# Two DMA queues for x and B, x transposed between the halves of B, and y one gate step later, in a fused state-space and gated-FFN kernel

## The chip, the cores and the metric

The kernel runs on one core of one Trainium2 chip. The metric is the time of one execution on the device in microseconds (us). A profiled run also has a span, from the first to the last instruction that the profile counts, which is about 2 us shorter. Every execution is sorted as fast or slow by its time and granted clock, and only fast ones are compared; the state of a single execution is unknown. Engines are named as in the profile: PE (matrix engine), DVE (vector), ACT (scalar), POOL (GpSimd) and SP (sync, which issues most DMAs).

## The reference, cut to what matters

```python
xn = _layernorm(x)                              # 2048 tokens x 512
Bu = xn @ B_bar.T                               # complex, 512 states
h[t] = Lam_bar * h[t-1] + Bu[t]                 # complex recurrence over 2048 tokens
s  = 2 * real(h @ C.T) + xn * Dskip
g  = silu((gelu(xn @ w_gate) * (xn @ w_up)) @ w_down)     # width 1376
out = x + s * g
```

## The kernel before

The tokens are worked in four slabs of 512. In each slab PE makes eight groups `u` (B times xn), which DVE rotates, scans and rotates back into `hst`; eleven gate steps `g_ps`, `up_ps`; four groups `f` (the down projection); and four groups `y` from `hst` (C times h). The `y` of slab s-1 stand between the gate steps of slab s, at the steps `Y_AT`. All tiles in PSUM, the memory that PE writes its results to, are taken in turn from eight buffers under one tag, so each PE group waits until the reader of the tile eight places earlier is done.

```python
psum = ctx.enter_context(tc.tile_pool(name="psum", bufs=8, space=bass.MemoryType.PSUM))
...
def ffn(s, j, at):                     # one gate step
    ...                                # 4 matmuls into g_ps, 4 into up_ps
    ACT(out=gt[:fs], in_=g_ps[:fs, :], func=AF.Gelu_apprx_tanh)
    ACT(out=ub[:fs], in_=u_ps[:fs, :], func=AF.Copy)
    dve(now() + 0.9, 0.34, lambda: TT(out=at[:fs, j, :], in0=gt[:fs], in1=ub[:fs], op=ALU.mult))
def down(s, m, at):
    ...                                # 11 matmuls into f_ps; ACT makes th = tanh(f/2)
    dve(now() + 0.9, 0.6, lambda: STT(out=g2[:], in0=th[:], scalar=1.0, in1=f_ps[:, :], op0=ALU.add, op1=ALU.mult))
def epi(s, m, y_ps, g2):
    ...                                # DVE: yg = y_ps * g2; ot = yg + x
    nc.sync.dma_start(out=out_td[mg : mg + P, :], in_=ot[:])
def ln_small(s):                       # 7 POOL instructions on 128x4: mean, variance, rs, nb
def ln_out(s, m):                      # ACT: xn = rs*x + nb; SP: DMA transpose of xn into xnT
...
for j in range(NFT):                   # slab s > 0
    ffn(s, j, ats[s])
    if s < NS - 1:
        if j < M: ln_act(s + 1, j)     # sums of the next slab's rows, on ACT
        if j == M - 1: ln_small(s + 1)
        if 5 <= j < 5 + M: ln_out(s + 1, j - 5)
    if j in Y_AT: ...                  # y of slab s-1 and its epilogue
```

DVE's instructions are ordered when the program is built, by a small model of PE's and DVE's clocks: `dve(ready, cost, f)` places an instruction at a modelled time, with the queued scans and rotations put in ahead of it where they fit. A model that is wrong costs time at run time, because the order is fixed.

## Time and profile before

| | before |
|---|---|
| time, median of 4 fast runs | 190.67 us (190.26 to 191.15) |
| span of the profiled run | 188.8 us |
| PE, DVE, ACT, POOL busy | 96%, 88%, 57%, 12% |
| first `u` matmul | 10.94 us |
| gaps of PE over 0.2 us after it | one: the first `y` of slab 1 (1.34 us lost) |

The page of the kernel before has, in its first part, the busy time of each engine (share of the span, number of instructions), and in its fourth part the engines' shares of the chain that ended last:

```profile
PE 181.2 (96%) x918; PEld 85.9 (45%) x918; DVE 165.5 (88%) x284; ACT 108.0 (57%) x202; POOL 21.7 (12%) x35
...
PE 89%; ACT 4%; DMA 2%; DVE 2%; SPq 1%; issue 0%
...
L431 DVE TENSOR_TENSOR at<-gt,ub 128x512 bf16<-128x512 bf16 (+1 forms) x44 | 18.2, 416 | 4.2 <-ACT ub L430 4.0
```

The last line is from the costliest groups: busy time, mean ns, and then the idle time of DVE just before these instructions, here 4.2 us, 4.0 of them ended by ACT's copy `ub`. PE rules the chain; DVE works 88% of the time.

### The profile page before, as it was taken

How to read it: one execution, taken by the hardware profiler on the slowest of the kernel's cores; microseconds unless marked ns; L12 is line 12 of the kernel's file. 1: busy time of each engine (PE TensorE's matmuls, PEld its weight loads, DVE VectorE, ACT ScalarE, POOL GpSimd, SP SyncE). 2: the span in 40 equal slices, each digit the busy share in tenths (PEclk: the TensorE clock that was granted, in tenths of full speed). 3: DMA queues.
4: the chain of work that ended last, by engine and by line, in shares of the span. 5: the costliest groups of instructions: out<-in, count | busy, mean ns of one | idle time of the engine just before them, and what ended most of it. 6: DMA issues, size and time to landing. Idle time of an engine off the chain costs nothing.

```text
span 188.8 us, 2587 instructions
## 1 busy us (share of the span) xinstructions
PE 181.2 (96%) x918; PEld 85.9 (45%) x918; DVE 165.5 (88%) x284; ACT 108.0 (57%) x202; POOL 21.7 (12%) x35
## 2 busy tenths in 40 slices
PE   7789999999999799999999999999999999999992
PEld 2444444444444244544444444544444444554452
DVE  4879799999999897999999999999999999973353
ACT  3399989995259919536239959537226644321210
POOL 3737200000000470000000080000000000000000
PEclk9999999999999999999999999999999999999999
DMA  5999948700000003300000003300000000000001
GB/s 131 343 363 360 233 110 254 109 3 0 0 0 0 0 3 84 82 28 28 0 5 0 0 2 83 87 28 28 0 0 0 3 0 28 28 28 31 28 30 56
DMA packets 21164, 12.26 MB, mean 65 GB/s; under 512 B 11456, under 2 KB 21152, under 8 KB 21152
## 3 DMA queue, kind: packets, MB, share of 16 engines
q1 hardware_dynamic: 20976, 12.03, 23.7%
q8 instruction: 7, 0.11, 0.2%
q10 hardware_dynamic: 176, 0.07, 0.1%
q14 instruction: 5, 0.04, 0.1%
HBM read 7.38 MB, written 2.10 MB: 50 GB/s over the span
## 4 chain that ended last, share of the span: by engine, by line
PE 89%; ACT 4%; DMA 2%; DVE 2%; SPq 1%; issue 0%
PE f_ps L438 20%; PE up_ps L423 18%; PE g_ps L418 18%; PE u_ps L333 15%; PE y_ps L457 14%; DMA Bn<-in_A_B_re_dram 2%; ACT junk L512 2%; PE y_ps L462 2%; PE tb_ps L140 1%; ACT ub L430 1%; PE y_ps L490 1%; SPq L89 1%; ACT gt L428 1%; DVE qq L352 1%; DVE xnT L212 0%; DVE hst L356 0%
## 5 line engine op out<-in xcount | busy, mean ns | idle before, releaser
L418 PE MATMUL g_ps<-xnT,wg 128*128 128x512 bf16 (+1 forms) x176 | 45.2, 379 | 0.0
L423 PE MATMUL up_ps<-xnT,wu 128*128 128x512 bf16 (+1 forms) x176 | 45.2, 379 | 0.0
L438 PE MATMUL f_ps<-wd,at 128*128 128x512 bf16 (+1 forms) x176 | 38.7, 379 | 0.0
L428 ACT ACTIVATE gt<-g_ps 128x512 bf16<-128x512 f32 (+1 forms) x44 | 26.0, 592 | 13.2 <-PE g_ps L418 13.2
L382 DVE TENSOR_TENSOR_SCAN Ft<-rho,it,Wt 128x512 bf16<-128x512 f32 x24 | 30.3, 1276 | 0.0
L457 PE MATMUL y_ps<-C,hst 128*128 128x512 bf16 x120 | 28.7, 379 | 1.0 <-DVE hst L356 1.0
L430 ACT ACTIVATE ub<-up_ps 128x512 bf16<-128x512 f32 (+1 forms) x44 | 26.3, 598 | 5.1 <-PE up_ps L423 5.1
L333 PE MATMUL u_ps<-xnT,BT 128*128 128x512 bf16 x128 | 28.3, 379 | 0.6 <-DVE xnT L212 0.6
L443 ACT ACTIVATE th<-f_ps 128x512 f32<-128x512 f32 x16 | 9.6, 598 | 32.3 <-PE f_ps L438 30.5
L423 PEld LDWEIGHTS <-wu 128*128 128x128 bf16 (+1 forms) x176 | 17.6, 100 | 20.4
L438 PEld LDWEIGHTS <-at 128*128 128x128 bf16 (+1 forms) x176 | 17.1, 98 | 20.6
L418 PEld LDWEIGHTS <-wg 128*128 128x128 bf16 (+1 forms) x176 | 17.2, 100 | 18.4
L338 ACT ACTIVATE U<-u_ps 128x512 bf16<-128x512 f32 x32 | 17.7, 602 | 8.3 <-PE u_ps L333 8.3
L431 DVE TENSOR_TENSOR at<-gt,ub 128x512 bf16<-128x512 bf16 (+1 forms) x44 | 18.2, 416 | 4.2 <-ACT ub L430 4.0
L333 PEld LDWEIGHTS <-BT 128*128 128x128 bf16 x128 | 12.4, 98 | 15.1 <-issue 0.7
L457 PEld LDWEIGHTS <-hst 128*128 128x128 bf16 x120 | 11.5, 98 | 15.1 <-DVE hst L356 2.0
L445 DVE SCALAR_TENSOR_TENSOR g<-th,f_ps 128x512 f32<-128x512 f32 x16 | 10.9, 679 | 7.6 <-ACT th L443 7.6
L527 ACT ACTIVATE xn<-x_tok,nb,rs 128x512 bf16<-128x512 bf16 x12 | 9.8, 814 | 6.1 <-POOL nb L523 6.1
L475 DVE TENSOR_TENSOR yg<-y_ps,g 128x512 bf16<-128x512 f32 x15 | 10.3, 684 | 1.9 <-PE y_ps L462 1.8
L356 DVE TENSOR_TENSOR Wt<-pp,qq 128x1024 bf16<-128x1024 bf16 x16 | 10.8, 688 | 0.3
L356 DVE TENSOR_TENSOR hst<-pp,qq 128x1024 bf16<-128x1024 bf16 x16 | 10.6, 689 | 0.2
L517 POOL TENSOR_SCALAR sx<-sx 128x4 f32<-128x4 f32 x2 | 1.4, 684 | 81.2 <-ACT junk L512 81.2
(108 smaller groups left out, 166.6 us busy)
## 6 DMA issues: line engine op xcount, KB each, us to landing
out_dram<-ot SPq DMA_DIRECT2D x15, 128.0 KB, 1.7
x_tok<-in_A_x_dram SPq DMA_DIRECT2D x3, 512.0 KB, 4.1
wd<-in_B_w_down_dram SPq DMA_DIRECT2D x1, 1280.0 KB, 11.3
x_tok<-in_A_x_dram SPq DMA_DIRECT2D x4, 128.0 KB, 2.4
Bn<-in_A_B_re_dram SPq DMA_DIRECT2D x1, 512.0 KB
Bn<-in_A_B_im_dram SPq DMA_DIRECT2D x1, 512.0 KB, 5.6
wg<-in_B_w_gate_dram SPq DMA_DIRECT2D x1, 512.0 KB, 8.2
wu<-in_B_w_up_dram SPq DMA_DIRECT2D x1, 512.0 KB
```

What stands on the lines that cost most here:

```text
L333: nc.tensor.matmul(u_ps[:, :], lhsT=BT[:, ri, kt, pt * P : (pt + 1) * P], rhs=xnT[:, kt, cols], start=(kt == 0), stop=(kt == KT - 1),)
L338: ACT(out=U[:, ri, q, :], in_=u_ps[:, :], func=AF.Copy)
L356: return lambda: TT(out=dst()[i], in0=box["pp"][:, i, :, :], in1=box["qq"][:, 1 - i, :, :], op=op)
L382: nc.vector.tensor_tensor_scan(out=box["F"][:, ri, q, :], data0=rho[:, pt : pt + 1].to_broadcast([P, TS]), data1=box["W"][:, ri, q, :], in ...
L418: nc.tensor.matmul(g_ps[:fs, :], lhsT=wg[:, kt, fsl], rhs=xnT[:, kt, cols], start=(kt == 0), stop=(kt == KT - 1))
L423: nc.tensor.matmul(u_ps[:fs, :], lhsT=wu[:, kt, fsl], rhs=xnT[:, kt, cols], start=(kt == 0), stop=(kt == KT - 1))
L428: ACT(out=gt[:fs], in_=g_ps[:fs, :], func=AF.Gelu_apprx_tanh)
L430: ACT(out=ub[:fs], in_=u_ps[:fs, :], func=AF.Copy)
L431: dve(now() + 0.9, 0.34, lambda: TT(out=at[:fs, j, :], in0=gt[:fs], in1=ub[:fs], op=ALU.mult))
L438: nc.tensor.matmul(f_ps[:, :], lhsT=at[:fs, k, m0 : m0 + P], rhs=wd[:fs, k, :], start=(k == 0), stop=(k == NFT - 1))
L445: dve(now() + 0.9, 0.6, lambda: STT(out=g2[:], in0=th[:], scalar=1.0, in1=f_ps[:, :], op0=ALU.add, op1=ALU.mult))
L457: nc.tensor.matmul(y_ps[:, :], lhsT=hst[:, j // NPT, j % NPT, m0 : m0 + P], rhs=C2[:, j // NPT, j % NPT, :], start=(j == 0), stop=False,)
```

## The change

It is meant to fill DMA capacity that lies unused at the start, to let DVE's work on x overlap the loads of B, and to give DVE one gate step more for `hst` before the first two `y`.

```diff
-    for m in range(M):
-        nc.sync.dma_start(out=x_tok[:, m, :], in_=x_r[:, m, :])
+    nc.sync.dma_start(out=x_tok[:, 0, :], in_=x_r[:, 0, :])
+    nc.sync.dma_start(out=x_tok[:, 1, :], in_=x_r[:, 1, :])
+    nc.sync.dma_start(out=x_tok[:, 2:M, :], in_=x_r[:, 2:M, :])
+    load_b(nc.sync, 1, A_B_im)
     for i, v in enumerate((A_log_dt, A_Lambda_im, A_Lambda_re, A_Dskip)):
         nc.scalar.dma_start(...)
-    for ri, src in enumerate((A_B_re, A_B_im)):
-        nc.sync.dma_start(out=Bn[:, ri, :, :], ...)
+        if i == 1:
+            load_b(nc.scalar, 0, A_B_re)
...
-    dummies(10) ... dummies(3)
+    dummies(12)
+    b_transposes(0)
...  (statistics and norms of x; x0 and x1 transposed; the parameters transposed)
+    b_transposes(1)
     nc.vector.tensor_copy(out=pf[:], in_=pt_ps[:, :])
...  (norms of x2, x3; copies to xnT; the angle chain now after them)
-    Y_AT = (5, 7, 9, 10)
+    Y_AT = (6, 8, 9, 10)
...
-    clk["pe"] = 9.5
+    clk["pe"] = 9.0
```

The last line is the start of the modelled clock.

More of the change, by code (lines that the diff above doesn't have):

```diff
@@ L87, with load_b @@
     wu_r = B_w_up.rearrange("(k p) f -> p k f", p=P)
-    for m in range(M):
-        nc.sync.dma_start(out=x_tok[:, m, :], in_=x_r[:, m, :])
+    def load_b(eng, ri, src):
+        eng.dma_start(out=Bn[:, ri, :, :], in_=src.rearrange("(k p) d -> p k d", p=P))
+    nc.sync.dma_start(out=x_tok[:, 0, :], in_=x_r[:, 0, :])
+    nc.sync.dma_start(out=x_tok[:, 1, :], in_=x_r[:, 1, :])
+    nc.sync.dma_start(out=x_tok[:, 2:M, :], in_=x_r[:, 2:M, :])
+    load_b(nc.sync, 1, A_B_im)
     for i, v in enumerate((A_log_dt, A_Lambda_im, A_Lambda_re, A_Dskip)):
         nc.scalar.dma_start(out=pv[4 * i : 4 * i + 4, :], in_=v.rearrange("(k p) -> k p", p=P))
-    for ri, src in enumerate((A_B_re, A_B_im)):
-        nc.sync.dma_start(out=Bn[:, ri, :, :], in_=src.rearrange("(k p) d -> p k d", p=P))
+        if i == 1:
+            load_b(nc.scalar, 0, A_B_re)
     cuts = [0, 3 * P, 7 * P, F]
@@ L181 @@
     ch = consts.tile(W3, BF16, name="ch")
-    dummies(10)
+    dummies(12)
+    b_transposes(0)
+    for a in (0, 2):
+        for m in (a, a + 1):
+            bn(0, m)
+        for m in (a, a + 1):
+            bn_end(0, m)
+        rstd(0, a, a + 2)
+    xs = [norm0(0), norm0(1)]
+    tps = [t_xn0(0, xs[0]), t_xn0(1, xs[1])]
     pt_ps = psum.tile([P, 16], BF16, name="pt_ps", tag="ps")
     nc.tensor.transpose(pt_ps[:, :], pv[:, :], ident[0:16, 0:16])
-    dummies(3)
-    bn(0, 0)
-    bn(0, 1)
-    bn_end(0, 0)
-    bn_end(0, 1)
-    rstd(0, 0, 2)
-    bn(0, 2)
+    b_transposes(1)
     nc.vector.tensor_copy(out=pf[:], in_=pt_ps[:, :])
     nc.gpsimd.tensor_tensor(out=dt_[:], in0=euler[:], in1=ldt, op=ALU.pow)
-    bn(0, 3)
-    bn_end(0, 2)
-    bn_end(0, 3)
-    rstd(0, 2, 4)
-    xs = [norm0(0), norm0(1)]
-    STT(out=thn[:], in0=lim, scalar=1.0 / (2.0 * math.pi), in1=dt_[:], op0=ALU.mult, op1=ALU.mult)
-    TT(out=a1[:], in0=lre, in1=dt_[:], op=ALU.mult)
-    nc.gpsimd.tensor_tensor(out=rho[:], in0=euler[:], in1=a1[:], op=ALU.pow)
-    b_transposes(0)
-    tps = [t_xn0(0, xs[0]), t_xn0(1, xs[1])]
     xs += [norm0(2), norm0(3)]
-    b_transposes(1)
     for m in range(2):
@@ L212 @@
         nc.vector.tensor_copy(out=xnT[:, :, m * P : (m + 1) * P], in_=tps[m][:, :, :])
+    STT(out=thn[:], in0=lim, scalar=1.0 / (2.0 * math.pi), in1=dt_[:], op0=ALU.mult, op1=ALU.mult)
+    TT(out=a1[:], in0=lre, in1=dt_[:], op=ALU.mult)
+    nc.gpsimd.tensor_tensor(out=rho[:], in0=euler[:], in1=a1[:], op=ALU.pow)
     TT(out=ang[:], in0=iota_f[:].unsqueeze(1).to_broadcast(W3), in1=thn[:].unsqueeze(2).to_broadcast(W3), op=ALU.mult)
```

## The prediction

> **What bounds the kernel now.** I read the page first: the matrix engine (PE) is busy 96% of the span and takes 89% of the chain that ended last; the vector engine (DVE) is busy 88%. Then the chain in order of time, the PE timeline around its gaps, the DVE timeline between them, and busy time by stretch.
>
> The chain at the start (start, duration, piece):
> ```profile
> 2.66 4.57 DMA Bn<-in_A_B_re_dram
> 7.22 0.05 issue
> 7.27 1.07 PE tb_ps L140 x16
> 8.34 0.45 PE tp L171 x8
> ...
> 8.80 1.07 PE tb_ps L140 x16
> 9.87 0.24 PE tp L171 x4
> ...
> 10.13 0.77 DVE xnT L212 x2
> 10.90 0.04 issue
> 10.94 7.07 PE u_ps L333 x32
> ```
> The end hangs on the load of B_re, issued at 2.66 behind four x loads and landed at 7.22. Useful matmuls begin at 10.94.
>
> DMA by half microseconds (busy of PE, PEld, DVE, ACT, POOL, then clock, DMA share, GB/s):
> ```profile
> 2.50:3.00 0.50, 0.50 (x3) 0.22 (x2) 0.23 (x1) 0.50 (x1) 0.00 (x0) 1.00 0.75 206
> 4.00:4.50 0.50, 0.50 (x3) 0.17 (x2) 0.50 (x3) 0.00 (x0) 0.00 (x0) 1.00 0.63 82
> 6.00:6.50 0.50, 0.00 (x0) 0.00 (x0) 0.47 (x5) 0.00 (x0) 0.50 (x1) 1.00 1.08 383
> ```
> The engines reach 383 GB/s only from 6 us on, with a hole of 82 GB/s at 4.0, between the end of x and the first bytes of B: bandwidth is unused before 5 us.
>
> PE timeline in slab 1, its only other gap:
> ```profile
> 63.62 0.59 PE L457 MATMUL y_ps<-C,hst 128*128 128x512 bf16 x2
> 65.17 1.68 PE L457 MATMUL y_ps<-C,hst 128*128 128x512 bf16 x6 [0.96 <-DVE hst L356]
> 66.69 0.39 PE L462 MATMUL y_ps<-diagI,xnT 128*128 128x128 bf16 x4
> 66.91 1.03 PE L418 MATMUL g_ps<-xnT,wg 128*128 128x512 bf16 x4
> ```
> The first y of slab 0 waits for hst. Without a wait it takes 1.95 us (in the chain: 1.73 + 0.22), here 66.91 - 63.62 = 3.29, so 1.34 us are lost.
>
> DVE timeline there and at the end:
> ```profile
> 62.83 0.43 DVE L431 TENSOR_TENSOR at<-gt,ub 128x512 bf16<-128x512 bf16 x1 [0.78 <-ACT ub L430]
> 63.17 1.22 DVE L352 TENSOR_TENSOR qq<-Ft,sin_b 128x2048 bf16<-128x2048 bf16 x1
> 64.42 0.69 DVE L356 TENSOR_TENSOR hst<-pp,qq 128x1024 bf16<-128x1024 bf16 x1
> ...
> 71.92 0.43 DVE L431 TENSOR_TENSOR at<-gt,ub 128x512 bf16<-128x512 bf16 x1 [1.21 <-ACT ub L430]
> ...
> 165.54 0.68 DVE L356 TENSOR_TENSOR hst<-pp,qq 128x1024 bf16<-128x1024 bf16 x1
> ```
> After the wait at 71.92 DVE runs with next to no gap to the last hst, done near 166.2; PE asks for it at 167.99. DVE is thus a near second bound. From 67 us to the last y, PE has no gap.
>
> **What the skill says.** (1) "DMA: Bandwidth & Descriptors", section "Issuing engines are not separate DMA queues": a second issuing engine only saves the sequencer's issue time, since all run on the same 16 engines. The trace has issues of 0.43 and 0.51 us for the two loads of B. (2) The same page, "Queues, rings and completion order": each engine alternates between queue rows it has work for, packet by packet. So B_re, on its own queue, should share with x rather than stand behind it; with nearly all packets on one queue before (20,976, against 176 on the parameters' queue), this trace cannot show that. (3) "TensorE: Matmul & The Clock Gate", Part 1: the array's clock is halved until about 4 us of activity. The trace agrees: the first ten dummies take 3.90 us, the last three 0.82. Twelve dummies keep the warm-up, so I expect warm matmuls as before.
>
> **Part 1, the two queues.** The B_re issue moves from 2.66 to about 1.6 (behind two parameter issues, 0.72 to 1.58), B_im's from 3.13 to about 2.2. If DMA runs near 345 GB/s from 2.6 us on, x's rest and B_re share it: about 1 MB in 3.0 us ends at 5.6; with 0.5 us for completion (estimate) B_re lands near 6.1 instead of 7.22. Between 2.5 and 5.5 the trace moved 0.69 MB against 1.03 at that rate, so B_im, which landed at 8.73 (3.13 + 5.6 to landing), gains 0.34 MB / 365 GB/s = 0.9 us or more: about 7.5.
>
> **Part 2, x between the halves of B.** Now DVE sets the pace. x0 still arrives for 2.77, x1 perhaps at 3.9 (3.70 before). From the DVE rows: statistics of x1 to 4.5; two aggregates and an add, 0.41, to 4.9; statistics of x2 and x3, 1.3, to 6.2; again 0.41, to 6.6; two norms, 0.65, to 7.3. PE has turned B_re by 7.2 (6.1 + 1.07), transposes x0 and x1 by 7.65 and the parameters by 7.85. The parameter copy now stands before norms 2 and 3: 7.95, norms to 8.65, xnT copies 0 and 1 to 9.35. B_im is turned from 7.9 to 9.0 and x2, x3 by 9.4, just in time; the last copies end near 10.05. First u near 10.1: **gain 0.8 us** (0.3 if B_re or x2:4 comes half a microsecond late). The angle chain follows the copies; it delays ACT by less than the slack it regains by 23 us, where ACT waits for PE again. Slab 0 has no PE gap, so the 0.8 reaches slab 1.
>
> **Part 3, y one step later.** The heading says two, but Y_AT goes from (5,7,9,10) to (6,8,9,10): the first two move by one step of 8 matmuls, 1.73 us. hst hangs on ub at 62.83, which moves with PE, so PE comes 1.73 us later against the same hst. 1.73 exceeds 1.34: the wait goes, with 0.4 to spare. **Gain 1.34 us**. PE's matmul count only changes by one dummy.
>
> **What it costs DVE.** The order of instructions in the built kernel shows qq, and then both Wt, around the `at` of step 6: that `at` now comes before both Wt and the y epilogue, where before one Wt and the epilogue preceded it. It still cannot start before ub at 71.92 minus the startup gain g (ACT waits for POOL's nb, 4.00 us). So Wt 0.6 and the epilogue 1.05 move behind the wait: 1.65 us more to do after it; one `at` (0.34) moves behind the last hst. Last hst: 166.2 + 1.65 - 0.34 - g = 167.5 - g. PE's last y needs it at its seventh matmul: 167.99 - 1.34 + 1.29 - g = 167.9 - g. Slack 0.4. PSUM has 8 buffers in rotation; the third y of a slab reuses the first's. In slab 1, first yg is done at 71.92 + 0.34 + 1.25 + 0.68 = 74.2 - g; PE wants the buffer at 53.42 + 10 x 1.73 + 2 x 1.95 = 74.6 - g. Again 0.4. By the same count slabs 2 and 3 come out at 0.3 to 0.7. All are hidden, but with margins no larger than my errors: I take off **0.25 us**.
>
> **Sum**: 190.75 - 0.8 - 1.34 + 0.25 = **188.9 us**, 1% less.
>
> **Rivals.** (a) The DMA is hidden or self-defeating: both halves of B interleave and land together near 8. Then the first transposes start at 8 and u at 10.9 or later, gain 0 or a loss of 0.3; y alone leaves 189.3 to 189.7. For it: the page on DMA, and rates near 1.0 DMA share already at 3.5 us. Against it: the hole at 4.0. (b) DVE becomes the bound, by late hst or late PSUM buffers, and gives back up to the 1.34: near 190. For it: 26.24 of 26.80 us busy in the last gate stage. Against it: the positive margins. (c) All margins hold and startup gains 1.3: 188.1. To pass 2% the time must fall below 186.9, 3.8 us; all gaps of PE after its first productive matmul are 1.34 us, so startup would have to give 2.5, and DVE's x chain alone forbids it.
>
> **Range and chances.** Startup 0.3 to 1.3, y 1.0 to 1.34, give-back 0 to 1: 187.9 to 190.1. Faster by over 2%: 0.02. Slower by over 2% needs 194.6, a new stall that no step shows: 0.01. Within 2%: 0.97.
>
> **What would show it.** Right: B_re landed near 6.1 and first u_ps near 10.1; no gap before y_ps in slab 1; the `at` of step 6 waiting longer than 1.21 (near 2.8); PE gaps in slabs 2 and 3 under 0.3 us. Wrong: first u after 10.6 (parts 1 and 2); PE waiting for yg or hst for over 0.5 us (the count of DVE's lag).

## The result

The changed kernel takes 193.22 us (median of 4 fast runs, 192.98 to 193.65) against 190.67 us. Ratios here are the mean time of one kernel's fast runs over that of the other's in the same rounds, so not quite the ratio of the medians. This one is 1.0136, with a 95% interval of 1.0104 to 1.0167: 1.4% slower, still within 2%, but outside the predicted range of 187.9 to 190.1. The spans are 191.3 and 188.8.

The same three places on the page of the changed kernel:

```profile
PE 181.2 (95%) x917; PEld 86.0 (45%) x917; DVE 164.8 (86%) x284; ACT 106.9 (56%) x202; POOL 23.2 (12%) x35
...
PE 57%; DVE 35%; DMA 2%; issue 2%; ACT 1%; SPq 0%; ACTq 0%; DVEq 0%
...
L431 DVE TENSOR_TENSOR at<-gt,ub 128x512 bf16<-128x512 bf16 (+1 forms) x44 | 18.1, 413 | 7.4 <-ACT ub L430 7.1
```

PE, DVE and ACT have no more work: PE's busy time is the same, DVE's is 0.7 us less and ACT's 1.1 us less. POOL's is 1.5 us more, with the same 35 instructions (below). But DVE holds 35% of the last chain instead of 2%, and its idle time before the products `at` grew from 4.2 to 7.4 us. So DVE stands still 3.2 us longer, and PE then waits for DVE.

**The start.** The chain in order of time (start, duration, piece) of the changed kernel:

```profile
1.64 4.70 DMA x_tok<-in_A_x_dram
6.34 0.02 issue
6.36 1.29 DVE st L156 x2
...
9.31 0.17 DVE pf L202
9.48 0.64 DVE xn L167 x2
10.13 0.66 DVE xnT L206 x2
10.79 0.67 DVE xnT L209 x2
11.47 0.04 issue
11.51 1.67 PE u_ps L333 x7
```

The chain no longer starts with B_re but with the load of x2 and x3, which takes 4.70 us. DVE's timeline shows the statistics of x2 and x3 before (one each):

```profile
4.72 0.69 DVE L151 BATCH_NORM_STATS2 st<-x_tok 128x6 f32<-128x512 bf16 x1
...
5.39 0.69 DVE L151 BATCH_NORM_STATS2 st<-x_tok 128x6 f32<-128x512 bf16 x1
```

and after, with the wait in brackets:

```profile
6.36 1.29 DVE L156 BATCH_NORM_STATS2 st<-x_tok 128x6 f32<-128x512 bf16 x2 [1.71 <-DMA x_tok<-in_A_x_dram]
```

B_re did land early: PE's first transposes of it start at 6.35. But x2 and x3, 256 KB on the other queue, landed with it (1.64 + 4.70 = 6.34), and DVE starts on them at 6.36. First `u` is at 11.51 instead of 10.94: 0.57 us lost.

**Slabs 1 to 3.** The PE timeline after, at the first `y` and at its three new gaps (idle time before and releaser in brackets):

```profile
65.05 1.03 PE L423 MATMUL up_ps<-xnT,wu 128*128 128x512 bf16 x4
65.91 1.89 PE L457 MATMUL y_ps<-C,hst 128*128 128x512 bf16 x8
...
102.22 1.03 PE L418 MATMUL g_ps<-xnT,wg 128*128 128x512 bf16 x4
103.77 1.02 PE L423 MATMUL up_ps<-xnT,wu 128*128 128x512 bf16 x4 [0.52 <-DVE g L445]
...
131.75 1.02 PE L333 MATMUL u_ps<-xnT,BT 128*128 128x512 bf16 x4 [0.99 <-DVE yg L475]
...
149.70 1.02 PE L423 MATMUL up_ps<-xnT,wu 128*128 128x512 bf16 x4 [1.37 <-DVE g L445]
```

The first `y` runs in one piece: its 1.34 us are saved, as predicted. A group of four matmuls starts 0.864 us after the one before it (in the chain of the kernel before, the eight groups `u` of slab 1 take 6.91 us), so the first gap costs 103.77 - 102.22 - 0.86 = 0.69 us. Reckoned the same way from 124.52, where the eight `u` groups begin, and from 147.30, the others cost 1.18 and 1.54. The sum is 3.41. The account is +0.57 - 1.34 + 3.41 = +2.64 us, against 2.5 us between the spans.

The groups that wait take a PSUM buffer for which a DVE reader is late: `up_ps` of step 3 reuses the buffer of the fourth `f_ps` (read by `g`), and the eighth `u` that of the fourth `y` (read by `yg`). DVE's rows before and after for this `g`, first before:

```profile
100.37 0.69 DVE L445 SCALAR_TENSOR_TENSOR g<-th,f_ps 128x512 f32<-128x512 f32 x1
```

then after, with the product `at` of step 6 in slab 2:

```profile
103.04 0.68 DVE L445 SCALAR_TENSOR_TENSOR g<-th,f_ps 128x512 f32<-128x512 f32 x1
...
113.25 1.22 DVE L352 TENSOR_TENSOR pp<-Ft,cos_b 128x2048 bf16<-128x2048 bf16 x1
116.69 0.43 DVE L431 TENSOR_TENSOR at<-gt,ub 128x512 bf16<-128x512 bf16 x1 [2.23 <-ACT ub L430]
```

This `g` ends 2.7 us later than before. The product of step 6 waits 2.23 us in slab 2, and likewise 2.23 in slab 1, where it waited 0.21 and 1.21 before. A product so far ahead in DVE's order stops all scans behind it.

**Why `ub` is late in slab 2.** ACT makes `xn` of the next slab ahead of it, and that waits for POOL's last instruction `nb`. ACT's row in slab 2, first before, then after:

```profile
112.80 0.82 ACT L527 ACTIVATE xn<-x_tok,nb,rs 128x512 bf16<-128x512 bf16 x1 [2.14 <-POOL nb L523]
```

```profile
114.87 0.81 ACT L527 ACTIVATE xn<-x_tok,nb,rs 128x512 bf16<-128x512 bf16 x1 [4.09 <-POOL nb L523]
```

POOL's seven instructions on 128x4 before (first, second and last):

```profile
108.04 0.39 POOL L517 TENSOR_SCALAR sx<-sx 128x4 f32<-128x4 f32 x1 [37.97 <-ACT junk L512]
108.51 1.02 POOL L518 TENSOR_TENSOR mq<-sx 128x4 f32<-128x4 f32 x1
...
112.54 0.23 POOL L523 TENSOR_SCALAR nb<-nb 128x4 f32<-128x4 f32 x1
```

and after:

```profile
108.16 1.29 POOL L517 TENSOR_SCALAR sx<-sx 128x4 f32<-128x4 f32 x1 [38.31 <-ACT junk L512]
...
113.37 1.15 POOL L522 TENSOR_TENSOR nb<-sx,rs 128x4 f32<-128x4 f32 x1
114.61 0.23 POOL L523 TENSOR_SCALAR nb<-nb 128x4 f32<-128x4 f32 x1
```

DVE's row that overlaps the first of these in the changed kernel:

```profile
108.16 1.28 DVE L382 TENSOR_TENSOR_SCAN Ft<-rho,it,Wt 128x512 bf16<-128x512 f32 x1
```

The chain takes 4.7 us before and 6.7 us after. In this slab the six simple instructions take 0.2 to 0.4 us when they are not held and 1.0 to 1.3 when a scan or a rotation product of DVE is under way (the power `rs` 1.1 or 1.9); the first one here ends with the scan, at 109.45 and 109.44. In the changed kernel four of the seven are lengthened in this way (1.29, 1.04, 1.89 and 1.15 us), before only two (1.02 and 1.89). The Trainium skill, "SBUF — State Buffer", section "Who interferes with whom", says that a DVE instruction with two SBUF inputs contends with a GpSimd instruction that reads SBUF, and that "Issue order, not op shape, decides who blocks". The rows agree for POOL: it is held until DVE's instruction ends. So a hundredth of a microsecond in the start of the chain could decide 2 us. So far this is a reading of rows; the experiments test it.

### The profile page after: what moved, and what is told of

Read it like the earlier page. It is cut to its first block, busy times and chain, and to the rows that moved or that the text cites. A ratio compares the mean times of both kernels' runs of the same rounds, so it can differ in the third digit from the quotient of the medians.

```text
span 191.3 us, 2583 instructions
## 1 busy us (share of the span) xinstructions
PE 181.2 (95%) x917; PEld 86.0 (45%) x917; DVE 164.8 (86%) x284; ACT 106.9 (56%) x202; POOL 23.2 (12%) x35
## 3 DMA queue, kind: packets, MB, share of 16 engines
q1 hardware_dynamic: 20432, 11.51, 22.6%
## 4 chain that ended last, share of the span: by engine, by line
PE 57%; DVE 35%; DMA 2%; issue 2%; ACT 1%; SPq 0%; ACTq 0%; DVEq 0%
PE up_ps L423 15%; PE g_ps L418 14%; DVE Ft L382 10%; PE f_ps L438 10%; PE y_ps L457 8%; PE u_ps L333 7%; DVE pp L352 5%; DVE qq L352 4%; DVE yg L475 3%; DVE g L445 2%; DMA x_tok<-in_A_x_dram 2%; DVE Wt L356 2%; DVE hst L356 2%; DVE at L431 2%; DVE ot L476 1%
## 5 line engine op out<-in xcount | busy, mean ns | idle before, releaser
L517 POOL TENSOR_SCALAR sx<-sx 128x4 f32<-128x4 f32 x2 | 2.3, 1136 | 81.7 <-ACT junk L512 81.7
L356 DVE TENSOR_TENSOR Wt<-pp,qq 128x1024 bf16<-128x1024 bf16 x16 | 10.6, 687 | 0.2
```

What stands on the lines that cost most here:

```text
L356: return lambda: TT(out=dst()[i], in0=box["pp"][:, i, :, :], in1=box["qq"][:, 1 - i, :, :], op=op)
```

## The experiments

All kernels gave correct results. Theory A blames the new places of `y`, with DVE's lag, and theory B the new start. Theory C is the race of POOL with the scan, and theory D is that B_re on the second queue delays x. "First u" is the start of the first `u` matmul in the profiled run.

### 1. Each part alone: e1_y_only, e2_start_only

```diff
 e1: kernel before
-    Y_AT = (5, 7, 9, 10)
+    Y_AT = (6, 8, 9, 10)
 e2: changed kernel
-    Y_AT = (6, 8, 9, 10)
+    Y_AT = (5, 7, 9, 10)
```

> The kernel before with only the y steps moved (5,7,9,10 to 6,8,9,10); its vector-engine order after the start is that of the changed kernel. Theory A (the moved steps make the vector engine late, and it frees PSUM buffers too late for the matrix engine in slabs 2 and 3; the start has no part in it): about 192.6 us, that is the changed kernel's 193.2 less the 0.57 us that its start lost; matrix-engine gaps of together about 3.4 us at gate step 3 of slabs 2 and 3 and at the last u group before slab 3, none at the first y. Theory B (the later start pushes the vector engine behind): no such gaps, 190.7 - 1.34 = 189.4 us.

> The changed kernel with the y steps put back to 5,7,9,10: the new start alone. Theory A: first u matmul at 11.5 us, the 1.3 us gap at the first y is back, no gaps in slabs 2 and 3: 190.7 + 0.57 = 191.3 us. Theory B (the start itself makes the vector engine late): the 3.4 us of gaps in slabs 2 and 3 remain and the time is 193 us or more.

The `y` alone: 190.84 us, ratio 0.9987 (0.9963 to 1.0011): nothing gained. Its gap of 1.34 us is gone, but PE waits 0.50 and 0.48 us for DVE's `g` at `up_ps` of step 3 in slabs 2 and 3, and first u came at 11.23. The start alone: 191.42 us, ratio 1.0016 (0.9992 to 1.0039), first u at 11.94, the gap of `y` back and none in slabs 2 and 3. Theory A gave 192.6 for the first and 191.3 for the second, theory B 189.4 for the first; neither part makes the loss of 2.5 us, so neither theory stands alone. The difference lies in slab 2. In e1 the product of step 6 waits 2.22 us in slab 1 but not in slab 2. POOL's first and last instruction and DVE's scan there, e1:

```profile
107.85 0.22 POOL L517 TENSOR_SCALAR sx<-sx 128x4 f32<-128x4 f32 x1 [38.28 <-ACT junk L512]
...
112.24 0.23 POOL L523 TENSOR_SCALAR nb<-nb 128x4 f32<-128x4 f32 x1
```

```profile
107.86 1.27 DVE L382 TENSOR_TENSOR_SCAN Ft<-rho,it,Wt 128x512 bf16<-128x512 f32 x1
```

Here POOL starts 0.01 us before the scan, takes 0.22 us, and its chain ends after 4.6 us.

### 2. The late product: e3_at6_ready, e4_ln_later

e3 has the changed kernel's product of step 6 placed 4.6 us of modelled time later in DVE's order. e4 leaves it and has ACT make `xn` at later steps, so that `ub` of step 6 does not stand behind it.

```diff
 e3: changed kernel
-        dve(now() + 0.9, 0.34, lambda: TT(out=at[:fs, j, :], ...))
+        late_at = 5.5 if j == 6 and 0 < s < NS - 1 else 0.9
+        dve(now() + late_at, 0.34, lambda: TT(out=at[:fs, j, :], ...))
 e4: changed kernel
-                    if 5 <= j < 5 + M:
-                        ln_out(s + 1, j - 5)
+                    for m in range(M):
+                        if j == (7, 7, 8, 8)[m]:
+                            ln_out(s + 1, m)
```

> The changed kernel, with the product of gate step 6 of slabs 1 and 2 told to the placing clock as ready 4.6 us later, so that both Wt and three scans stand before it on the vector engine. Theory A1 (the lag comes from the 2.23 us that the vector engine idles at that product, twice): these idles vanish, the gaps of the matrix engine in slabs 2 and 3 fall from 3.4 to under 1 us, time 190 to 191 us. Rival A2 (the lag comes from y standing later by itself, whatever the idle): gaps remain near 3 us, time 193 us.

> The changed kernel with the layer norm's output of the next slab moved from gate steps 5,6,7,8 to 7,7,8,8, so that ACT does the two evacuations of steps 6 and 7 before it waits for POOL. Theory A1: the vector engine's 2.23 us idles at the product of step 6 go to under 0.4, matrix-engine gaps in slabs 2 and 3 under 1 us, time near 190.3 us. Rival A2: time 193 us. Risk: the transposed rows arrive late for the next u group, a new gap of up to 1 us before u.

e3: 189.84 us, ratio 0.9937 (0.9913 to 0.9960). e4: 190.10 us, ratio 0.9967 (0.9916 to 1.0018). In both profiles the waits of the product are gone and PE has no gap after its first `u`, which starts at 11.41 and 11.53. POOL's chain in slab 2 still takes 6.5 us in e3 (107.16 to 113.68), so it was not made shorter; it only stopped costing anything. So the chain POOL `nb`, ACT `xn`, ACT `ub`, DVE `at`, DVE `g` and `yg`, PE is cut at either of two places, and the 3.4 us go with it. e3 is the first version clearly faster than both kernels; e4's interval still includes no change against the kernel before.

### 3. The race by itself: e5_race, e9_memset

e5 delays the start of POOL's chain by a tiny ACT copy (about 0.1 us) ahead of the last row sums, in the kernel with `y` alone, thus with the old start. e9 is meant to delay DVE's scan instead, by one small memset in the changed kernel.

```diff
 e5: kernel before, Y_AT = (6, 8, 9, 10)
     def ln_act(s, m):
+        if s == NS - 1 and m == M - 1:
+            ACT(out=tiny[:], in_=halfpi[:], func=AF.Copy)
 e9: changed kernel, in the scan's function
+                if (s, h, q, ri) == (2, 0, 0, 1):
+                    nc.vector.memset(scr[:], 0.0)      # 128x1
```

> The y-only kernel plus one tiny ACT copy (about 0.1 us) before the last statistics of slab 3's rows, so that POOL's first small instruction in slab 2 starts about 0.1 us later against the vector engine. In the y-only run that instruction started 0.01 us before a scan and took 0.22 us; in the changed kernel it started with the scan and took 1.29, and POOL's chain in slab 2 took 6.7 instead of 4.6 us. Theory C (the 2.4 us between the y-only and the changed kernel are this race of POOL against the vector engine's reads): POOL's chain takes 6 us or more, ACT waits about 4 us for nb in slab 2, the product of step 6 in slab 2 waits near 2.2 us, time 192.5 to 193 us instead of 190.8. Rival (the later start makes the difference): 190.9 us.

> The changed kernel with one memset of a 128x1 scratch added on the vector engine in slab 2, just ahead of the scan that POOL's first small instruction loses against. It takes some 0.06 us, so that POOL should start first. Theory C: that POOL instruction takes about 0.22 instead of 1.29 us, POOL's chain 4.6 instead of 6.7, ACT's wait for nb 2.0 instead of 4.1, and the added instruction makes the kernel faster: 193.2 to about 191.2 us. Rival: 193.2 us or a little more.

e5: 193.19 us, ratio 1.0116 (1.0037 to 1.0194), with the old start and first u at 10.35. POOL's first and last instruction, and DVE's scan:

```profile
107.82 1.20 POOL L519 TENSOR_SCALAR sx<-sx 128x4 f32<-128x4 f32 x1 [38.39 <-ACT junk L514]
...
114.18 0.23 POOL L525 TENSOR_SCALAR nb<-nb 128x4 f32<-128x4 f32 x1
```

```profile
107.73 1.27 DVE L382 TENSOR_TENSOR_SCAN Ft<-rho,it,Wt 128x512 bf16<-128x512 f32 x1
```

The race is lost by 0.09 us, the chain takes 6.6 us, ACT waits 4.00 us for `nb`, the product of step 6 waits 2.22 us in slab 2, and PE has gaps of 0.51, 0.71 and 1.38 us at the same three places as the changed kernel. e9 adds an instruction and is faster: 191.55 us, ratio 1.0050 (1.0030 to 1.0071), against 1.0136 without it. Its POOL row and DVE rows:

```profile
107.95 0.22 POOL L520 TENSOR_SCALAR sx<-sx 128x4 f32<-128x4 f32 x1 [38.30 <-ACT junk L515]
```

```profile
107.96 1.28 DVE L385 TENSOR_TENSOR_SCAN Ft<-rho,it,Wt 128x512 bf16<-128x512 f32 x1
107.99 0.06 DVE L381 MEMSET scr<- 128x1 f32 x1
```

The race is won by 0.01 us, ACT waits 2.04 us for `nb`, and two gaps of 0.52 and 0.51 us are left. How the memset won it is not shown: the scan's row still starts 0.32 us after the product before it, as in the changed kernel (107.64 to 107.96, and 107.84 to 108.16), and the memset's row starts after the scan's. But all four fast runs of e9 (191.15 to 191.66) lie under all four of the changed kernel. Theory C holds in both directions by outcome, and e5 shows it in the rows too: losing the race costs a kernel with these places of `y` about 2 us (193.22 - 191.55 = 1.67 and 193.19 - 190.84 = 2.35, of runs in different rounds).

### 4. The start: e6_one_queue, e7_x_split

```diff
 e6: changed kernel; B_re back on the first queue, after x
-        if i == 1:
-            load_b(nc.scalar, 0, A_B_re)
+    load_b(nc.sync, 0, A_B_re)        # between x2:4 and B_im
 e7: changed kernel; two queues, x2 and x3 in two loads
-    nc.sync.dma_start(out=x_tok[:, 2:M, :], in_=x_r[:, 2:M, :])
+    nc.sync.dma_start(out=x_tok[:, 2, :], in_=x_r[:, 2, :])
+    nc.sync.dma_start(out=x_tok[:, 3, :], in_=x_r[:, 3, :])
```

> The changed kernel with B_re's load put back on the first queue, between x2:4 and B_im: one queue, x2 and x3 still in one load. Read from it: when the statistics of x2 start (6.36 us in the changed kernel) and the first u matmul (11.5). Theory D (B_re on the second queue takes bandwidth from x2:4): statistics near 4.9, first u near 10.2 to 10.6. Rival E (the merged 256 KB load is what comes late): statistics still near 6.3, first u near 11.4.

> The changed kernel with x2 and x3 in two loads again, B still on two queues. Theory D: statistics of x3 still start near 6 us, first u 11 us or later. Rival E: statistics of x2 near 4.7 and x3 near 5.4 as before, first u near 10.3.

DVE's statistics of x2 and x3 in e6:

```profile
4.68 1.29 DVE L155 BATCH_NORM_STATS2 st<-x_tok 128x6 f32<-128x512 bf16 x2
```

and of x1, x2 and x3 in e7:

```profile
4.21 0.69 DVE L157 BATCH_NORM_STATS2 st<-x_tok 128x6 f32<-128x512 bf16 x1 [0.60 <-DMA x_tok<-in_A_x_dram]
5.36 0.69 DVE L157 BATCH_NORM_STATS2 st<-x_tok 128x6 f32<-128x512 bf16 x1
...
6.46 0.69 DVE L157 BATCH_NORM_STATS2 st<-x_tok 128x6 f32<-128x512 bf16 x1 [0.40 <-DMA x_tok<-in_A_x_dram]
```

With B_re off the second queue, x2 and x3 are there without a wait at 4.68, against 6.36. With two queues, even a load of their own does not bring x3 before 6.4. So sharing the DMA engines with B_re delays x, as theory D has it. The other profiles repeat it: in the eight with two queues and x2:4 in one load (after, e2, e3, e4, e8, e9, e15, e17) these statistics start at 6.17 to 7.07 and always wait for the load; with one queue (e6 here, and e11 and e12 below) they start at 4.62 to 4.97 and never do. First u is 10.50 in e6 and 11.00 in e7. In e6 the race was lost (first POOL instruction 1.29 us), in e7 won (0.22), though only the loading of x and B differs: a change of the start can also turn the race, by hundredths of a microsecond.

### 5. A shorter POOL chain: e8_pool5

```diff
 changed kernel: 1/D and the sign go into ACT's scale of the row sums
-        G.tensor_scalar(out=mean, in0=mean, scalar1=1.0 / D, ...)
...
-        G.tensor_scalar(out=var, in0=var, scalar1=1.0 / D, scalar2=EPS, op0=ALU.mult, op1=ALU.add)
+        G.tensor_scalar(out=var, in0=var, scalar1=EPS, ...)      # after the subtraction
-        G.tensor_scalar(out=nb[:, s, :], in0=nb[:, s, :], scalar1=-1.0, ...)
```

> The changed kernel with POOL's chain for the next slab's layer norm cut from 7 to 5 small instructions (the factors 1/D and the sign go into ACT's sums). Theory A1 with C: the chain gets 1 to 2 us shorter in slabs 1 and 2, ACT's wait for nb with it, the product of step 6 waits 0.5 to 1.5 us instead of 2.23, the matrix engine's gaps in slabs 2 and 3 fall to under 1 us: 190.3 to 191 us. Rival A2 (y's new place alone makes the lag): 193 us.

191.61 us, ratio 1.0039 (0.9964 to 1.0113). ACT's waits for `nb` are 1.44 and 2.88 us, and the product of step 6 still waits 0.44 and 1.91 us; one PE gap of 1.12 us is left, at 148.13. Five instructions help, but the chain stays exposed to DVE.

### 6. Better starts on one queue: e10_oneq_at6, e11_x_first, e12_all

e10 is e6 with the late product of e3. e11 also normalizes and transposes all of x ahead of B_im. e12 adds e8's POOL chain.

```diff
 e11, against e10
-    b_transposes(1)
-    (pf copy, dt)
     xs += [norm0(2), norm0(3)]
+    tps += [t_xn0(2, xs[2]), t_xn0(3, xs[3])]
+    b_transposes(1)
+    (pf copy, dt)
```

> The two things that helped, together: one queue for x and B (first u at 10.50 us in its one look, against 11.41 in the run with the product of step 6 told as late) and that late product. If they add: 189.84 - 0.9 = 188.9 us, first u near 10.5, no matrix-engine gap over 0.3 us after it. If the start is swallowed by a later wait: 189.8 us.

> As the run before it, with all four x tiles normalized before the parameter copy and transposed before B_im. The vector engine no longer waits 1.2 us for the parameters, and the copies to xnT of x2 and x3 no longer wait for B_im: first u near 10.0 instead of 10.5, time 188.4 us. If instead u's second group then waits for the evacuation of B_im: no gain, 188.9 us.

> As the run before it, with POOL's chain of five instead of seven instructions. If with the late product POOL's chain is off the path: same time within 0.2 us, 188.4. If it still held anything back: up to 0.5 us less. If the shorter chain moves the race to a worse phase: 189 us or more.

e10: 190.52 us, ratio 0.9988 (0.9962 to 1.0014); its profiled run was slow (clock 0.991), so its profile is not used. e11: 189.73 us, ratio 0.9957 (0.9939 to 0.9975). e12: 189.71 us, ratio 0.9959 (0.9932 to 0.9985). The expected 188.9 for e10 and 188.4 for e11 were missed. In e11 B_im landed at 9.22 and in e12 at 9.91, where PE waited for it, while in e6 it had landed by 8.37: on one queue the start hangs on B_im, and its landing moves by more than the gain. A new wait also appears, 0.59 and 0.84 us before `u` of slab 3. e12's shorter POOL chain changed nothing.

### 7. The old start without DVE's lag: e13_y_at6, e14_y_at6_pool5, e15_at6_again

```diff
 e13: kernel before, with Y_AT = (6, 8, 9, 10) and e3's late_at
 e14: e13 with e8's POOL chain
 e15: e3 again, on the same chip
```

> The old start with the new places of y and the late product of step 6: does the new start earn anything once DVE's lag is gone? If the new start costs what its first u says (theory D: x2:4 delayed by B_re, 0.3 to 0.6 us), this kernel loses no gap of y (1.34 us gained) and comes to 190.7 - 1.34 = 189.3 us, below the repeated late-product kernel with the new start (189.8). If the new start is worth something after all (rival), it comes to 190.0 or more. In the profile: no gap of PE over 0.2 us before up_ps or u_ps in slabs 1 to 3, no wait near 2.2 at the product of step 6.

> The same with POOL's chain of five instructions. If late products of step 6 have taken all waits of DVE away already, the shorter chain gives nothing more: 189.3 +- 0.2, waits for nb near 1.4 us at most. If the chain's place (lock with DVE) still costs, it is 0.3 us or more faster than its twin.

> Repeat of the changed kernel with the late product of step 6 on this chip, for the comparison with the old start: 189.8 us, ratio near 0.994, first u near 11.5.

e13: 189.98 us, ratio 0.9961 (0.9943 to 0.9980). e14: 190.03 us, 0.9966 (0.9938 to 0.9994). e15: 189.79 us, 0.9950 (0.9934 to 0.9965). The expected 189.3 of e13 was missed, and its rival's number, 190.0, came out. So by the medians the old start is worth nothing over the new one. The profiles do not settle it: first u was 10.07 in e13 and 11.90 in e15, but e15's profiled run was the slowest of its six (191.66; the other five 189.61 to 190.36), so it is not typical. What both profiles show is a new wait before `u`: 0.41 us in slab 1 and 0.82 us in slab 3 in e13, 1.24 us in slab 3 in e15 (and 0.99 in e14). All wait for DMA transposes `xnT<-xn`. Around slab 3 the sync queue's rows of e13 are (start, duration of the issues, what):

```profile
113.80 2.86 SPq L530 DMA_TRANSPOSE xnT<-xn  x2
118.71 0.33 SPq L480 DMA_DIRECT2D out_dram<-ot  x1
119.14 3.46 SPq L530 DMA_TRANSPOSE xnT<-xn  x2
```

and PE, e13:

```profile
123.96 7.07 PE L333 MATMUL u_ps<-xnT,BT 128*128 128x512 bf16 x31 [0.82 <-DMA xnT<-xn]
```

The store of the first output, issued only when DVE has made `ot`, stands between the second and the third transpose in the program. ACT had finished the third `xn` at 117.12, but its transpose was issued only after the store, at 119.14.

### 8. The store behind the transposes: e16_store_later, e17_store_later_new

e16 is e13, and e17 is e15, with that store issued after the fourth transpose.

```diff
+        if m == 0 and s < NS - 2:
+            held.append(store)
+        else:
+            store()
...
                     if 5 <= j < 5 + M:
                         ln_out(s + 1, j - 5)
+                        if j == 4 + M and held:
+                            held.pop()()
```

> Old start, new places of y, late product of step 6, and the store of a slab's first output issued after the fourth transpose of xn instead of between the second and the third. In e13 the sync engine held the third and fourth transposes behind that store (118.71) until 119.14, and u of slab 3 waited 0.82 us for them. If that queue order is the cause (theory), the transposes are issued right after their xn (near 117.2 and 118.9), no gap before u is left, and the time falls by 0.8 us against e13, to 189.2 or under. Rival: the transposes are slow by themselves on this chip, the gap stays and the time stays at 190.0.

> The same with the new start. u of slab 3 waited 1.24 us in e15's profiled run (191.66 us), none in e3. With the wait gone in all runs the median falls to 189.3 or so and the spread with it (e15: 189.61 to 191.66). Against e16 it tells what the new start is worth: nothing, if both are within 0.3 us.

The sync queue of e16:

```profile
113.57 7.33 SPq L535 DMA_TRANSPOSE xnT<-xn  x4
120.99 6.53 SPq L481 DMA_DIRECT2D out_dram<-ot  x4
```

PE has no gap over 0.2 us after its first `u` in either kernel. e16: 189.41 us, ratio 0.9925 (0.9897 to 0.9954), the lowest ratio of all kernels here, and its expected 189.2 or under was missed by 0.2. e17: 190.18 us, ratio 0.9955 (0.9931 to 0.9980), no gain on e15's 0.9950: so the wait it removes does not seem to have limited the median of e15. On one chip the medians of the two starts now differ by 0.77 us, though the intervals of the two ratios overlap. The PE timeline of e17's profiled run (its slowest, 190.66) shows where such a difference lies:

```profile
7.41 1.07 PE L145 MATMUL tb_ps<-ident,Bn 128*128 128x128 bf16 x16 [1.35 <-DMA Bn<-in_A_B_re_dram]
...
12.21 7.07 PE L333 MATMUL u_ps<-xnT,BT 128*128 128x512 bf16 x32 [0.79 <-DVE xnT L209]
```

First u is 12.21 there and 10.42 in e16's profiled run (its fastest, 188.81), so these two overstate it. Over the profiled runs, the old start had first u at 10.07 to 11.23 (before, e1, e5, e13, e14, e16; mean 10.59), the new one at 11.32 to 12.21 (after, e2, e3, e4, e8, e9, e15, e17; mean 11.73).

## Why the prediction was wrong

**Part 1, two queues: half right.** B_re landed near 6.1 as predicted (6.35), and B_im at 7.9 (2.18 + 5.7) against 7.5. That the second queue brought B_re forward is not shown, though: PE's transposes of B_re began at 6.12 to 7.41 in the nine profiles with two queues (mean 6.72), and at 6.55, 6.78 and 7.02 in e6, e11 and e12, with one queue and B_re behind all of x. Less was unused than the three rows of the prediction suggest: the same view shows 306 and 271 GB/s from 3.0 to 4.0 us, and 379 from 5.5. Its 0.5 us for completion is an assumption that no trace here was read for. But rival (a)'s sharing took place one load earlier than it said: not B_re and B_im, but x2:4 and B_re landed together.

**Part 2: the step that failed** is "statistics of x2 and x3, 1.3, to 6.2". They began at 6.36 and ended at 7.65, because x2:4 came at 6.36. The step had x's arrival unchanged although it made B_re share the engines with x. First u came at 11.51 instead of 10.1, a loss of 0.57 us in place of a gain of 0.8. The text allowed 0.3 of gain if x2:4 came half a microsecond late, but not the 1.7 us that DVE waited.

**"Slab 0 has no PE gap, so the 0.8 reaches slab 1"** is not safe either. e13, with first u at 10.07, waits 0.41 us before `u` of slab 1, and e5, with 10.35, waits 0.57 us; both wait for the transposes of slab 1's `xn`. Of the 0.87 us that e13 is earlier than before at first u, 0.30 are left at `u` of slab 1 (36.54 against 36.84). e16, with 10.42, has no such wait (36.32). So a start as early as predicted may lose part of its gain there.

**Part 3: right.** The wait at the first `y` vanished. Where all new waits are removed and the old start is kept (e16), the median is 1.40 us under that of before in the same rounds (190.81 to 189.41), against 1.34 predicted. The closeness is partly luck: the interval of its ratio stands for 0.9 to 2.0 us, and first u varies too.

**What it costs DVE: the mechanism was right, the term mis-sized**, 0.25 us against 3.41. Three things were wrong in it. First, the count of PSUM: it took the third `y` for the tight place, and "by the same count slabs 2 and 3 come out at 0.3 to 0.7". The tight ones are the eighth `u`, behind the fourth `y`, and `up_ps` of step 3, behind the fourth `f_ps`; the rows name `yg` and `g` as releasers. Second, "near 2.8" for the wait at the product of step 6 was about right (2.23 in slab 1), but the count added it up for slab 1 only, while its delay went on to `g` of the next slab: e1, where the product waits in slab 1 only, still has gaps of 0.50 and 0.48 us. Third, POOL's chain was taken to move with PE unchanged. It lost 2 us to DVE's instructions in slab 2, so the product waited 2.23 us there too; e5 and e9 show this by switching it on and off. Rival (b), that DVE becomes the bound and PSUM buffers come late, was the right rival in kind, but it was capped at giving back the 1.34; the measured give-back is two and a half times that. Both signs of being wrong that the prediction named came true: first u after 10.6, and PE waiting for `yg` for over 0.5 us (0.99).

**What was luck.** That the changed kernel lost the race in slab 2 by so little, and e7 with nearly the same start won it, is chance as far as these runs show. But with the race won, e9 still takes 191.55 us and not 188.9, so the start and the missing count of `g` and `yg` remain wrong even then.

**What stays open.** First u varies by over 1 us between runs of one start with the landing of B, and no run here says why. The new start is 1.1 us later on average at first u, but its price in time was between nothing (e13 and e15) and 0.8 us (e16 and e17), and a profile shows first u of one run only. Why the third and fourth transposes took 3.46 us to issue in e13 and 2.5 us in e1 and e3 is open too; e3 had the same store between them and no gap, so the store alone does not make one.

## What to carry to other kernels

A gain on one engine that makes another engine wait once more must be followed through every shared buffer: list, for the rotation of PSUM tiles, which reader frees the tile of each group, and take the tightest one. An instruction that waits for a slow chain should stand as late in its engine's order as its consumer allows; moving one product was worth 3.4 us here. Before a load goes to a second queue, ask which load on the first one it will delay, and before a start is made earlier, what the next stage's inputs wait for.

## What the Trainium skill lacked or had wrong

- "SBUF — State Buffer", "Who interferes with whom": the rule agrees with POOL's side of the runs, but it gives no size for tiny GpSimd instructions. A 128x4 instruction of 0.22 us took 1.20 to 1.29 us behind a scan, a chain of seven grew from 4.6 to 6.7 us, and the order of two starts 0.01 us apart went with it. Where POOL came first (107.85 against 107.86), the scan still took 1.27 us, so no block of DVE by POOL shows in its rows.
- "DMA: Bandwidth & Descriptors", "Issuing engines are not separate DMA queues": it says that DMAs of several engines interleave, and that issuing from more than one only saves issue time. Here it also cost time: x2:4 landed at 6.34, where with one queue it was usable by 4.68. How the engines shared is not shown: 256 KB on one queue and 512 KB on the other landed together, at 6.34 and about 6.35.
- No page gives a size or an example for a DMA transpose behind a store that is not ready on the same issuing engine: 0.82 us before `u` in e13, none in e16.
- No page has a word on a PSUM rotation of mixed kinds, where a late reader of one kind (`g`, `yg`) stops matmuls of another (`up_ps`, `u_ps`): 3.41 us in the changed kernel.
